# A fused attention and gated-MLP kernel: small steps moved off GpSimd, dependent pairs planned apart, tables offered to ScalarE

## The chip, the cores and the metric

The kernel runs on one core of one Trainium2 chip. The metric is the time of one execution in device microseconds; the time before is the median of three runs. A core has five instruction queues that matter here: TensorE (PE: matrix products, with its weight loads shown as PEld), VectorE (DVE), ScalarE (ACT), GpSimd (POOL) and SyncE (SP), which issues the DMA transfers. Each works through its own queue in order and waits on semaphores for the others.

## What is computed

Windowed causal attention with a distance penalty, whose output is the input of a gated MLP with a mix over the sequence. Batch 8, 8 heads, sequence 576, head size 64; model width 512, inner width 1024.

```python
scores = q @ k.T / sqrt(D) - slope[h] * (i - j)      # only 0 <= i - j < 128
attn = softmax(scores)
x = concat_heads(attn @ v)
u, v = split(relu(x @ w_in))
v_n = (v - mean(v)) / sqrt(var(v) + 1e-06)
out = (u * (w_spatial @ v_n + b_spatial)) @ w_out
```

## The kernel before, in words

The program is written as a list of pieces. Each piece (`plan.add`, `plan.either`) has an engine, or several to choose from, a weight (its planned time in ns), a due time, and the tiles that it reads and writes. `Plan.order` (L190) then simulates the engines with these weights: a piece that becomes ready goes to the engine whose queue, free time and weight end first (L207 to L211); a free engine takes the ready piece with the smallest number in the table `PLACES` (one three-digit hexadecimal number per piece, 2707 of them). `Plan.emit` (L259) writes the instructions out in that order, so the order on each engine is fixed before the program runs; no engine reorders anything. Where the simulated TensorE idles in the opening, `fill` (L388) puts matmuls of ones that compute nothing into a score bank (`x`, second buffer).

The work comes in stages that the plan overlaps:

- **Constants** (`constants`, L394). GpSimd writes the distances i - j of a tile (`relf`, and the transposed `relT`) in 64 rows; VectorE copies them to the other 64 (L401, L428). From them come eight tables `tabs` (L433 to L441, slope times distance, one per head; VectorE, and GpSimd from the third on, may make them) and eight transposed ones (L449, ScalarE or VectorE).
- **Opening attention** (`turned`, L740) for the four head pairs of batch 0 and two of batch 1. Scores go to PSUM (L720), VectorE adds the table and takes each row's extreme (L761), `split` (L764) cuts that number into three bf16 parts with two dependent subtractions (GpSimd or VectorE), TensorE transposes them (L779), and a second, transposed set of scores with table and maximum added by products (L791) gives the exponentials (L811). They are multiplied with v (L820); VectorE adds a small number to the row sums and inverts them (L847, L848, the second needs the first), and the output is scaled (L852 or L858), transposed (L865) and split into two f16 parts `xt` (L455, L877).
- **Attention of the other head pairs** (`scores`, `products`, `attention`, L893 to L1032): scores, table and extreme on VectorE (L914), exponentials (L920), division into two f16 parts (L952, L957), a DMA transpose (L963), and the products with v (L996).
- **Scales.** Weights and v are scaled by a power of two before they are cut into two f16 parts. `largest` (L640) finds the greatest sum of absolute values of v (L700 sums on ScalarE, one instruction per head pair); `scale_of` (L662) clamps it and multiplies it with two constants on GpSimd (L669, L670), then VectorE masks exponent bits (L672, L673). There are twelve scales: eight for v, four for weights (`column_scale`, L512).
- **Gated part** (`gated`, L1058), for each batch: products with w_in (L1081, L1103, L1132), the layer norm (`layer_norm`, L1038: statistics, their combination at L1046, variance plus epsilon at L1047, the power -1/2 on GpSimd at L1051, the normalization at L1055), the mix over the sequence (L1153), the gate, and the product with w_out (L1185).
- **Mixing weights** (`mixing_weights`, L578): the bias row is scaled into `r2` at rows 64 and 96, and its rounding error is put at row 96 (L633 to L636).

Of the kernel before, what the change touches and what calls it, by code (L numbers as in the profile page):

```python
# [21 lines left out]
def _as_f32(bits):  # L22
# [9 lines left out]
    "00000200100800501a00700400b0851e000601800901f01604301904203e06f03b07106007a05b07c00300c01201002e03005705003801401b01c02102202802702c02f034"  # L32
    "03903f08704404003c05905f04804f05405d06706c0700771991ad00a00e00d01100f01301501d01702301e02502402b02903102002602a03203302d03603a03d04a04c051"
    "05505a05205c06306606803704904104504704b04e06203504604d05305805606406106d07607d08408a08d08008608e09309505e06e06a06506b07307407906907207507e"
    "08107808c0830970a30b00b80bb0c00a50a80af0b20bd07b08208908f09209109b09d0c50ce0d20dd0e30e40d10d80df0e50e707f09609c0a2a920880900ad0b40c10c70b3"
    "0ae0e00b50c30bc0bf0c60cd0d40ca0d00db0e10e90ea0f10f70fa1d811511e13f1481041131020fc0ba0c40cc0d60f21011030ee0f80fb10010610810d1100fe10910e112"
    "11611a12412c0e80ed0f00f50fd10710b10511811d12712d1301361391111171201261d612b13313813c12313413714214a14e15315c13513e14414d15215615d160166168"
    "16914614f14b15713b13d14516717517f15416115e16a16416e17017c18718b14014314917217918117d18318218d1a21a818919119519b1d71961b01a51be1bb1c51c21c6"
    "1db19219f1b11b81981af1a31ae1b41ba1b61c41c11c81f71fa1c71e21ff2031d01e32001e71f822722b1f520b21f1fc20e22321022422922c21b22e24223124124e236246"
    "25124b2583402522633470f30990a009f0a40a70ac0ab0b70c20eb0ef0f41eb0f908b09409809e09a0a10a90a60b10b60b90be0c90c80cb0d50d70f610a10f11912212910c"  # L40
    "11b12112a12e0aa0cf0d30dc0d90da0de0e20e60ec0ff11411f12511c13212f13a15015b16c1e81fb1901ab1b51e51ec12813114c15115516315916b16216f14715815a174"
    "14115f17316d17816517617717b17e1801a01a419319419c1a119719d19e1aa1cd1b21c318a18c19a1cf1a91d91841881ee17117a1861a71d31da1851a61d11d51d41dc18f"
    "1b718e1ac1c91cc1d21ca1ce1bd1cb1e11e41e91f11e61ef1ea1f21ed1f41f01f620920721220a21320c21420420d20120f22f1f91fe20523923c23723a1b91df1bc1f31b3"
    "1fd1c021123324c26726c27546a1bf1dd20622520821822022d22223021621a21922a21e22621c22120221521721d23423823b23f24024723d24524824a24324925a24d253"
    "25b25f25e26025025925625c27123223524424f25525425727325d26d27827d28128628828b26a28428728a28c29129429a29e2a32a427728f29229829c2a12a52aa28e2a8"
    "2b22b62b92bf2c32c929f2af2b82bc2c12c62c82cd35c2ac2b72b42c02ba2c72c42d02cb2d92d32f232c3362de2fe2f930833233830331133333a30d31c31532634e351322"
    "34532a34f38c39034a35e38f39335736637436337239139536e37938e3763853a937e39839d3a038839f3af3a53b53d43ad3bb3d83b93d74943c13db49a1de228276280264"
    "26926226626527926827c27228226f27e26e27a26127026b27428528928d2902932962972a62992a029529d2bd2ad2b02be2c229b2a72a22a92ab2ae2d223e27b27f2832cc"
# [1268 lines left out]
```

## Time and profile before

| | before |
|---|---|
| median of three runs | 550.13 us (547.89 to 550.28) |
| the profiled execution's own time | 549.31 us |
| its span, first to last instruction | 547.6 us |
| busy: PE, DVE, ACT, POOL | 536.4, 444.2, 393.5, 61.5 us |
| mean granted TensorE clock | 1.000 of full speed |

Busy time is the time in which at least one instruction of an engine ran. The trace also lists, for each group of instructions, the idle time of the engine in front of it and which engine's instruction ended it, and a chain of waits that leads back from the last instruction to the first.

### The profile page before, as it was taken

What the parts mean: (1) busy time and instruction counts of PE and PEld (TensorE: products, weight loads), DVE (VectorE), ACT (ScalarE), POOL (GpSimd) and SP (SyncE); (2) the same over time, 40 slices, a digit from 0 to 9 for tenths busy, and PEclk for the clock granted to TensorE, in tenths of its full rate; (3) what the DMA queues carried; (4) which work ended last, traced back from release to release, by engine and by line L of the source; (5) the groups of instructions that cost most, each with busy time, mean ns of one, the idle gap of its engine ahead of it and who ended that gap; (6) DMA issues with size and microseconds to landing.
All of it is one profiled execution on the core that took longest, in us unless ns stands there. A gap on an engine that the chain in (4) does not pass through costs nothing.

```text
span 547.6 us, 19207 instructions
## 1 busy us (share of the span) xinstructions
PE 536.4 (98%) x7753; PEld 395.2 (72%) x7753; DVE 444.2 (81%) x1622; ACT 393.5 (72%) x1219; POOL 61.5 (11%) x138
## 2 busy tenths in 40 slices
PE   7898999999999999999999999999999999999997
PEld 6787567775678857886687758886688857884775
DVE  9788999999999799778998599858997799625540
ACT  4567799998978788569977699759976787323212
POOL 4011320212210011100100011100220011001000
PEclk9999999999999999999999999999999999999999
DMA  8949430489979975958498666965564744610002
GB/s 252 326 159 323 114 99 31 95 170 205 239 127 216 205 164 115 197 144 184 119 192 168 167 137 133 197 165 140 106 141 118 153 89 89 87 65 24 2 12 76
DMA packets 161405, 78.67 MB, mean 144 GB/s; under 512 B 124834, under 2 KB 155554, under 8 KB 161316
## 3 DMA queue, kind: packets, MB, share of 16 engines
q1 hardware_dynamic: 161316, 77.45, 62.4%
q8 instruction: 60, 0.98, 0.7%
q14 instruction: 29, 0.24, 0.1%
HBM read 37.13 MB, written 9.44 MB: 85 GB/s over the span
## 4 chain that ended last, share of the span: by engine, by line
PE 84%; DVE 6%; ACT 6%; issue 1%; DMA 1%; POOL 0%; DVEq 0%; ACTq 0%
PE m L1153 18%; PE m L1185 16%; PE m L1132 15%; PE m L1081 13%; PE s L720 8%; PE x L996 7%; PE s L791 2%; PE m L1103 2%; PE x L390 2%; DMA moved<-pq 1%; PE x L820 1%; ACT prob L920 1%; ACT prob L858 1%; ACT vt L459 1%; PE x L865 1%
## 5 line engine op out<-in xcount | busy, mean ns | idle before, releaser
L920 ACT ACTIVATE prob<-prob,stat 128x192 f32<-128x192 f32 (+1 forms) x260 | 109.3, 424 | 9.5 <-DVE stat L914 9.1
L1153 PE MATMUL m<-wsp,staged 128*128 128x288 f16 x768 | 113.2, 286 | 0.0
L1132 PE MATMUL m<-xt,win 128*128 128x288 f16 x768 | 100.1, 286 | 0.3 <-ACT vt L459 0.3
L1185 PE MATMUL m<-gs,wout 128*128 128x288 f16 x768 | 99.2, 286 | 0.0
L952 ACT ACTIVATE pq<-prob,stat 128x192 f16<-128x192 f32 (+1 forms) x260 | 88.8, 420 | 9.6 <-DMA moved<-pq 3.0
L957 DVE SCALAR_TENSOR_TENSOR pq<-prob,stat,pq 128x192 f16<-128x192 f32 (+1 forms) x260 | 87.8, 379 | 3.5 <-ACT pq L952 3.2
L1132 PEld LDWEIGHTS <-win 128*128 128x128 f16 x768 | 74.8, 98 | 21.8 <-issue 1.8
L1153 PEld LDWEIGHTS <-staged 128*128 128x128 f16 x768 | 74.2, 98 | 21.1 <-issue 2.5
L1185 PEld LDWEIGHTS <-wout 128*128 128x128 f16 x768 | 74.5, 98 | 20.3 <-issue 1.4
L914 DVE CUSTOM_DVE_ANT_0 prob<-s,tab 128x192 f32<-128x192 f32 (+1 forms) x260 | 71.6, 318 | 19.1 <-PE s L720 18.8
L1081 PE MATMUL m<-win,xt 128*128 128x512 f16 x384 | 86.3, 380 | 0.7 <-ACT o L1191 0.5
L1081 PEld LDWEIGHTS <-xt 128*128 128x128 f16 x384 | 36.4, 98 | 46.2 <-issue 5.4
L1051 POOL TENSOR_TENSOR st<-st,nhalf 128x1 f32<-128x1 f32 (+1 forms) x40 | 27.5, 687 | 296.5 <-DVE st L1047 290.3
L1161 DVE TENSOR_TENSOR u<-m,u 128x288 f32<-128x288 f32 x64 | 28.8, 449 | 35.2 <-PE m L1153 35.0
L720 PE MATMUL s<-qkraw 64*64 64x64 f32 (+1 forms) x1116 | 53.6, 313 | 1.5 <-DVE most L761 1.5
L920 ACT ACTIVATION_READ_ACCUMULATOR prob<-prob,stat 128x1 f32 (+1 forms) x260 | 49.6, 191 | 0.0
L1191 ACT ACTIVATE o<-m,am 128x288 f32<-128x288 f32 x41 | 20.2, 496 | 40.0 <-PE m L1185 32.8
L720 PEld LDWEIGHTS s<-qkraw 64*64 64x64 f32 x1116 | 40.3, 133 | 4.3 <-DVE most L761 1.9
L996 PEld LDWEIGHTS <-vh 128*64 128x64 f16 (+1 forms) x1664 | 34.6, 111 | 8.1 <-issue 6.6
L996 PE MATMUL x<-moved,vh 128*64 128x64 f16 (+1 forms) x1664 | 39.3, 197 | 0.1
L459 ACT ACTIVATE u<-m 128x288 f32<-128x288 f32 x54 | 21.7, 404 | 24.4 <-PE m L1132 24.1
L996 PE MATMUL x<-moved,vl 128*64 128x64 f16 (+1 forms) x832 | 37.4, 195 | 0.0
(167 smaller groups left out, 760.8 us busy)
## 6 DMA issues: line engine op xcount, KB each, us to landing
qkraw<-in_qk_dram SPq DMA_DIRECT2D x28, 576.0 KB, 4.3
vb<-in_v_dram SPq DMA_DIRECT2D x32, 320.0 KB, 5.7
out_dram<-o SPq DMA_DIRECT2D x64, 144.0 KB, 2.0
staged<-in_w_in_dram SPq DMA_DIRECT2D x8, 512.0 KB, 7.5
moved<-in_w_out_dram SPq DMA_DIRECT2D x4, 512.0 KB, 5.9
gw<-in_w_spT_dram SPq DMA_DIRECT2D x4, 288.0 KB, 7.5
moved<-pq SPq DMA_TRANSPOSE x52, 4.7
qkraw<-in_qk_dram SPq DMA_DIRECT2D x2, 320.0 KB, 4.6
```

Of the source, the lines that this page charges most:

```text
L720: nc.tensor.matmul(sc[j]()[out, at:at + k1 - k0], raw()[rows, 0, i * D:(i + 1) * D], raw()[rows, 1, k0:k1], start=True, stop=True, skip_gr ...
L914: nc.vector.tensor_tensor_reduce(pt(), sc[t][j]()[:m, SOFF[t]:SOFF[t] + n], tabs[h]()[:m, W - n:], -0.125, 3e38, ALU.add, ALU.min, st()[:m ...
L920: nc.scalar.activation(pt(), pt(), AF.Exp, bias=st()[:m, NM, j, t:t + 1], scale=-1.0, accum_out=st()[:m, SM, j, t:t + 1])
L952: nc.scalar.activation(pq[j]()[:m, 0, qs], prob[2 * (p % 2) + j]()[:m, cs], AF.Copy, scale=st()[:m, RC, j, t:t + 1])
L957: nc.vector.scalar_tensor_tensor(pq[j]()[:m, 1, qs], prob[2 * (p % 2) + j]()[:m, cs], st()[:m, RC, j, t:t + 1], pq[j]()[:m, 0, qs], ALU.mu ...
L996: nc.tensor.matmul(xp()[j * D:(j + 1) * D, x0:x0 + D], l()[rows, kt, j * D:(j + 1) * D], rhs, start=(i % 2, j) not in seen, stop=False, sk ...
L1051: nc.gpsimd.tensor_tensor(st()[:m, 11:12], st()[:m, 10:11], nhalf()[:m], ALU.pow)
L1081: nc.tensor.matmul(pt(), xt[c]()[:, X0[a] + t * P:X0[a] + (t + 1) * P], win()[:, c, w, DH:DF], start=(n == 0), stop=(n == 3 * NC_ - 1))
L1132: nc.tensor.matmul(pt()[:, :HS], win()[:, c, w, d * P:(d + 1) * P], xt[c]()[:, X0[a] + hf * HS:X0[a] + (hf + 1) * HS], start=(n == 0), sto ...
L1153: nc.tensor.matmul(pt()[:, :HS], l, r, start=(n == 0), stop=(n == len(ops) - 1))
L1161: nc.vector.tensor_tensor(u(), pt()[:, :HS], u(), ALU.mult)
L1185: nc.tensor.matmul(pt()[:, cs], wout()[:, d, w, e * P:(e + 1) * P], gs[d]()[:, a, cs], start=(n == 0), stop=(n == 3 * ND - 1))
```

## The change

Two subtractions of `split` and the two steps of `scale_of` move from GpSimd to VectorE. Pairs of small operations of which the second needs the first (in `split`, `scale_of`, after L820, and in the layer norm) become two pieces each, so that the plan can put other work between them. The copies of the distances and the eight tables may also go to ScalarE. For batches 1 to 7 the absolute sums of v take two head pairs per instruction, and `junk` doubles. The bias row lies at rows 64 and 65 instead of 64 and 96 and is scaled in one instruction. Some planned weights change, and the table of places has 2764 entries instead of 2707. In the diff unchanged lines and the table are left out.

```diff
@@ -29,65 +29,67 @@
...
@@ -358,7 +360,7 @@
-    junk = fixed([P, NQ * P], F16, "junk")
+    junk = fixed([P, 2 * NQ * P], F16, "junk")
@@ -398,7 +400,8 @@
-        plan.add("DVE", 500, 800, lambda: nc.vector.tensor_copy(relf()[D:], relf()[:D]), [(relf, 0)], [(relf, 1)])
+        plan.either([("DVE", 400, lambda: nc.vector.tensor_copy(relf()[D:], relf()[:D])), ("ACT", act(W), lambda: nc.scalar.copy(relf()[D:], relf()[:D]))],
+                    800, [(relf, 0)], [(relf, 1)])
@@ -425,7 +428,8 @@
-        plan.add("DVE", 575, 1000, lambda: nc.vector.tensor_copy(relT()[D:], relT()[:D]), [(relT, 0)], [(relT, 0)])
+        plan.either([("DVE", 400, lambda: nc.vector.tensor_copy(relT()[D:], relT()[:D])), ("ACT", act(W), lambda: nc.scalar.copy(relT()[D:], relT()[:D]))],
+                    1000, [(relT, 0)], [(relT, 0)])
@@ -438,7 +442,10 @@
-            plan.either([("DVE", 420, fv)] + [("POOL", pool(W), f)] * (h > 1), 1000 + h * 1000, [(relf, 0), (relf, 1)], [(tabs[h], 0)])
+            def fs(h=h):
+                slope = 2.0 ** (-8.0 * (h + 1) / H)
+                nc.scalar.activation(tabs[h](), relf(), AF.Copy, scale=-8.0 * slope)
+            plan.either([("DVE", 420, fv), ("ACT", act(W), fs)] + [("POOL", pool(W), f)] * (h > 1), 1000 + h * 1000, [(relf, 0), (relf, 1)], [(tabs[h], 0)])
@@ -485,7 +492,7 @@
-        return lambda: plan.add("DVE", dve(n), due + 3, f, [*W, X], [X])
+        return lambda: plan.add("DVE", dve(n) + 60, due + 3, f, [*W, X], [X])
@@ -589,7 +596,7 @@
-            nc.sync.dma_start(bt()[96:97, :], b_sp)
+            nc.sync.dma_start(bt()[65:66, :], b_sp)
@@ -630,11 +637,16 @@
-        def f():
-            for a in (64, 96):
-                nc.vector.tensor_scalar(r2()[a:a + 1, :], bt()[a:a + 1, :], sc(a, a + 1), None, ALU.mult)
-            nc.vector.scalar_tensor_tensor(r2()[96:97, :], bt()[96:97, :], sc(96, 97), r2()[96:97, :], ALU.mult, ALU.subtract)
-        plan.add("DVE", 1950, due + 2600, f, [(rest_, 1), (r2, 2), (r2, 1)] + ready, [(r2, 1)])
+        def fv():
+            nc.vector.tensor_scalar(r2()[64:66, :], bt()[64:66, :], sc(64, 66), None, ALU.mult)
+        def fa():
+            nc.scalar.activation(r2()[64:66, :], bt()[64:66, :], AF.Copy, scale=sc(64, 66))
+        plan.either([("DVE", 530, fv), ("ACT", act(S, 1), fa)], due + 2600, [(rest_, 1), (r2, 2), (r2, 1)] + ready, [(r2, 1)])
+        def f():
+            nc.vector.scalar_tensor_tensor(r2()[64:65, :], bt()[64:65, :], sc(64, 65), r2()[64:65, :], ALU.mult, ALU.subtract)
+        plan.add("DVE", dve(S, pointers=1) + 100, due + 2601, f, [(rest_, 1), (r2, 1)] + ready, [(r2, 1)])
@@ -666,9 +678,12 @@
-            nc.gpsimd.tensor_scalar(am()[:, 2:3], am()[:, col:col + 1], 2.0 ** -98, 2.0 ** 126, ALU.max, ALU.min)
-            nc.gpsimd.tensor_scalar(am()[:, 3:5], consts(), am()[:, 2:3], None, ALU.mult)
-        plan.add("POOL", 850, due, f, [(am, key), (consts, 0)], [(am, 3)])
+            nc.vector.tensor_scalar(am()[:, 2:3], am()[:, col:col + 1], 2.0 ** -98, 2.0 ** 126, ALU.max, ALU.min)
+        plan.add("DVE", 75, due, f, [(am, key)], [(am, 5)])
+        def f():
+            nc.vector.tensor_scalar(am()[:, 3:5], consts(), am()[:, 2:3], None, ALU.mult)
+        plan.add("DVE", 130, due, f, [(am, 5), (consts, 0)], [(am, 3)])
@@ -696,10 +711,13 @@
+        z = 2 if b else 1
+        for p in range(0, NP, z):
-                nc.scalar.activation(junk().rearrange("p (a b) -> p a b", b=P), vb()[:, p, :, 1:1 + P], AF.Abs, accum_out=am()[:, 8 + p:9 + p])
-            plan.add("ACT", act(NQ * P, 1), due + 8000 + p * 100, f, [(vb, p)], [(junk, 0), (am, ("sum", p))])
-        largest(am, [(am, ("sum", p)) for p in range(NP)], lambda: am()[:, 8:8 + NP], due + 9000, b < ONPE)
+                nc.scalar.activation(junk()[:, :z * NQ * P].rearrange("p (a b) -> p a b", b=P), vb()[:, p:p + z, :, 1:1 + P].rearrange("p c a b -> p (c a) b"), AF.Abs,
+                                     accum_out=am()[:, 8 + p // z:9 + p // z])
+            plan.add("ACT", act(z * NQ * P, 1), due + 8000 + p * 100, f, [(vb, p + k) for k in range(z)], [(junk, 0), (am, ("sum", p))])
+        largest(am, [(am, ("sum", p)) for p in range(0, NP, z)], lambda: am()[:, 8:8 + NP // z], due + 9000, b < ONPE)
@@ -761,10 +779,10 @@
-        def split(e):
-            for k in range(2):
-                e.tensor_tensor(ms()[:, :, :, k + 1], ms()[:, :, :, k], upper()[:, :, :, k], ALU.subtract)
-        plan.either([("DVE", 420, lambda: split(nc.vector)), ("POOL", 800, lambda: split(nc.gpsimd))], due + 2500, MS, [MR])
+        for k in range(2):
+            def split(k=k):
+                nc.vector.tensor_tensor(ms()[:, :, :, k + 1], ms()[:, :, :, k], upper()[:, :, :, k], ALU.subtract)
+            plan.add("DVE", 100, due + 2500 + k, split, MS if k == 0 else [MR], [MR])
@@ -845,8 +863,11 @@
+                plan.add("DVE", 110, d, f, [(xp, 0), (am, 4)], [(sm, 1)])
+                def f(sm=sm, nt=nt):
-                plan.add("DVE", 345, d, f, [(xp, 0), (am, 4)], [(sm, 0)])
+                plan.add("DVE", 105, d + 1, f, [(sm, 1)], [(sm, 0)])
@@ -1044,8 +1065,11 @@
+        plan.add("DVE", 100, due + 2, f, [(st, 0)], [(st, 3)])
+        def f():
-        plan.add("DVE", 335, due + 2, f, [(st, 0), (am, 12)], [(st, 1)])
+        plan.add("DVE", 110, due + 2, f, [(st, 3), (am, 12)], [(st, 1)])
@@ -1053,7 +1077,7 @@
-        plan.add("DVE", dve(DH, True, 2), due + 4, f, [(vt, 0), (st, 1), (st, 2)], [(vt, 0)])
+        plan.add("DVE", dve(DH, True, 2), due + 4, f, [(vt, 0), (st, 3), (st, 2)], [(vt, 0)])
```

## Rows read from the trace of the kernel before

**Rows 1.** The page, busy time: busy us, share of the span, instructions.
```profile
PE 536.4 (98%) x7753; PEld 395.2 (72%) x7753; DVE 444.2 (81%) x1622; ACT 393.5 (72%) x1219; POOL 61.5 (11%) x138
```

**Rows 2.** Stretches: from:to, length, busy us of each engine, PEclk, DMA share, GB/s.
```profile
0.00:60.00 60.00, 54.30 (x1125) 42.83 (x1126) 50.50 (x206) 36.51 (x80) 12.66 (x43) 1.00 0.86 267
60.00:120.00 60.00, 59.92 (x793) 43.06 (x795) 57.95 (x177) 56.83 (x165) 11.09 (x19) 1.00 0.35 82
120.00:480.00 360.00, 358.85 (x5285) 263.47 (x5278) 309.94 (x1179) 284.19 (x942) 34.99 (x72) 1.00 0.74 153
480.00:548.00 68.00, 63.36 (x561) 45.86 (x559) 25.85 (x62) 16.02 (x33) 2.78 (x5) 0.99 0.10 36
```

**Rows 3.** Line 390, the fillers: ns min/median/max, starts; idle before, by releaser.
```profile
L390 PE MATMUL x<-ones x131: 243/246/368, 1.3 to 58.2; 128*128 128x192 bf16 x131
...
  ACT prob L858: 1.4, 1
```

**Rows 4.** The chain of waits in order of time: start us, us, what.
```profile
43.46 1.81 PE x L390 x20
...
58.87 2.60 PE m L1081 x12
```

**Rows 5.** Timeline, 3 to 9 us: start, us, engine, line, operation, [idle before].
```profile
3.47 3.99 DVE L440 TENSOR_SCALAR tab<-u 128x192 bf16<-128x192 f32 x8
...
4.50 0.50 PE L720 MATMUL s<-qkraw 64*64 64x64 f32 x6
...
5.26 1.58 POOL L885 MEMSET pq<- 128x384 f16 x6
...
7.38 0.35 DVE L761 CUSTOM_DVE_ANT_0 s<-s,tab 128x192 f32<-128x192 f32 x1
...
8.67 0.74 ACT L700 ACTIVATE junk<-vb 128x640 f16<-128x640 f32 x1 [3.07 <-DMA vb<-in_v_dram]
...
8.84 0.58 PE L720 MATMUL s<-qkraw 64*64 64x64 f32 x3 [1.50 <-DVE most L761]
```

**Rows 6.** Lines 440 and 449, the tables: ns min/median/max, first and last start.
```profile
L440 DVE TENSOR_SCALAR tab<-u x8: 241/314/1809, 3.5 to 7.2; 128x192 bf16<-128x192 f32 x8
...
L449 ACT ACTIVATE gs<-u x8: 345/346/362, 3.5 to 5.3; 128x192 bf16<-128x192 f32 x8
```

**Rows 7.** Line 766, the splits: ns min/median/max; then busy us, mean ns.
```profile
L766 POOL TENSOR_TENSOR most<-most x10: 207/208/1235, 10.5 to 57.1; 128x10 f32<-128x10 f32 x10
...
L766 DVE TENSOR_TENSOR most<-most x2: 181/182/183, 13.3 to 13.5; 128x10 f32<-128x10 f32 x2
...
L766 POOL TENSOR_TENSOR most<-most 128x10 f32<-128x10 f32 x10 | 4.2, 421 | 30.1 <-DVE most L761 21.4 <-DVE sm L847 8.3
```

**Rows 8.** Scales: lines 669, 670, 672 (ns min/median/max); timeline at 40 us.
```profile
L669 POOL TENSOR_SCALAR am<-am x8: 209/229/971, 16.6 to 402.4; 128x1 f32<-128x1 f32 x8
...
L670 POOL TENSOR_SCALAR am<-powers,am x8: 313/314/2278, 16.9 to 403.5; 128x2 f32<-128x2 f32 x8
...
L672 DVE TENSOR_SCALAR am<-am x8: 132/144/155, 19.4 to 403.9; 128x1 int32<-128x1 int32 x8
...
39.97 0.31 POOL L670 TENSOR_SCALAR ham<-powers,ham 128x2 f32<-128x2 f32 x1
...
41.26 0.14 DVE L672 TENSOR_SCALAR ham<-ham 128x1 int32<-128x1 int32 x1
```

**Rows 9.** Timeline of VectorE at 67 us: two pairs, L847 and L848.
```profile
67.26 0.22 DVE L847 TENSOR_SCALAR sm<-x,am 128x6 f32<-128x6 f32 x1
67.52 0.19 DVE L848 RECIPROCAL sm<-sm 128x6 f32<-128x6 f32 x1
67.62 0.18 DVE L847 TENSOR_SCALAR sm<-x,am 128x4 f32<-128x4 f32 x1
```

**Rows 10.** Lines 700, 603 and 635: ns min/median/max, first and last start.
```profile
L700 ACT ACTIVATE junk<-vb x32: 719/734/824, 8.7 to 383.9; 128x640 f16<-128x640 f32 x32
...
L603 ACT ACTIVATE wsp<-gw x2: 1182/1188/1193, 48.4 to 50.3; 128x1152 bf16<-128x1152 f32 x2
...
L635 DVE TENSOR_SCALAR r<-moved,wam x2: 519/534/549, 64.8 to 65.4; 1x576 f16<-1x576 f32 x2
```

More of the change, by code (lines that the diff above doesn't have):

```diff
@@ L31 @@
 PLACES = (
[L32 to L47, printed above, removed]
@@ L88 @@
[L88 to L90 removed]
+    "00000400200601a01300300f01409c1fb00701b00801d01c04401704604107504007706608806408b00100901100e03903705905d03401502102502901e02702a02d031033"
@@ new lines @@
+    "03603a03b09d03d04e04a06c06905505c06807d07307608008419b1a400500d00a00b00c01201001601901802002202602402c02803e04201f02302b03002f02e035032038"
+    "03f04304805205806104c05005605b06206303c04904504d04b05105405706004704f05305a05f05e06a06707207907c07f08608f09307b08308508909009506506e06b06f"
+    "06d07407107a08207007807e08d08a08109209409709f0ad0b00bb0bf0c60a00a30aa0b80bc0c408708e09109b0a109a0a60a70cc0d50db0e30e60e90eb0d60d90e00e50ea"
+    "0ed08c09809e0a20abacb0a40960bd0c80c90cf0c70c30f30b50be0ba0c20cb0d10da0d40de0e20e70ef0f10f60f80fc1011f013213a15615e11412012a1301060d00d30d7"
@@ new lines @@
+    "0dd0e410d10f0f510310510910b1121171211220ff10e11111911d12612c1311360fa0fe10210710c11811b11312713313513913d14014714a12312812e1341381ef13c141"
+    "13e14612f14814e15415d16616c17717e14415015515f16316b16e17617c18518b18814d16515c1731531581611911a01a717018718318f18a19419319e1a91ad160162169"
+    "18618e19619a1ab1a51b01c81cf1af1b81bc1c31c61ed1c71d01d21d91d71e01de1e31f61b51c41c91cd1c21d11cb1d61e11e41d41dd1da1e61ff2071e21f220120b1eb1fd"
+    "21d1f720d22022c20220e22121922824022223723b23e22f24825c24325b26a24b26026f2652763672712883601040a90a50b20ac0b60c00ce0f40fb10010a2091100990a8"
@@ new lines @@
+    "0b30af0b70ae0b40b90c10c50ca0cd0d20d80dc0df0ee0ec10811511a12512b14b15111c11f12412d15215b0b10e10f70f20e80f00fd0f911611e12913713b14314513f14c"
+    "14f16417218c1a21ac1fe20417417817b18021821b14214915a17115916716f18917919217519716817f15718419817a19016a18118219519919d1a11a619f1a31ba1be1ae"
+    "1b21b91bb1e51a81aa1b31b61b11b41bf1c11cc1e820616d17d1ec1f318d1c51c01e719c1ca1e91ee1b71ce1bd1f51f81f11f41f91fa1df1ea1fc20020320f20821320c216"
+    "20521120a21522b22322d21a22421f22721c23022523124921721e2382532562512541d31d51d81dc21222a24d26726b27a28528a4a51db21022e23622623223a23f23d241"
@@ new lines @@
+    "23523c22923424424723323924224524624a24e25225525926226425d26325725f25a26127826c27027427b26926d26626827927d29224c24f25e26e27527227729827c290"
+    "29529c29f2a22a72aa2ad28d29e2a12a62a82ac2b22b72ba2c12c82c92962b12b52b92bd2c02c62ca2d02b32ce2e32ef2f12f62fc3003042c32d32f32f72f82fa2fe303305"
+    "3882d12da2d52e42dd2ff2e730630231330931b34c35131732231d32f34e35332933a35d36233434433f35e36c37134836e36437b3ad3b03723833bb3be37f38d3a8389395"
+    "3bd3c139239f3c739a3b63c33a23bc3c03c23bf3ca3e63c63d43f33cf3e83fc3d93f74b73ef4004bd21425028328928428f27328028128729329a28e29427f28c28629727e"
@@ L91 @@
+    "a21a12a16a1ba1ea259d49d79dca2ba2ca2da2ea27a2aa2fa48a4aa46a49a50a4ca51a52a54a56a57a59a5ba5ea4fa55a58a5aa5ca5fa61a62a64a67a69a6ba53a60a63a66"
+    "a68a6aa6ca6ea70a5da6da73a75a76a79a7fa82a85a65a71a78a7aa7ca7da80a84a86aa5a6fa74a72a7ba77a81a7ea87a83a89a88a8ba97a98a8aa8da8ca8fa9aa9da8ea91"
+    "a9ba9fa90a93a92a95a9eaa0a94a99a96aa1ab2ab5a9caa4ab4ab8aa2aa8aafaa6aaaab6abaaa9aadab7aabab0abeaaeab3ab9abcab1abbac1abdabfac4ac0ac2ac7ac3ac5"
+    "ac9ac6ac8aca"
 )
```

83 lines of the change are left out of this document (40 added, 43 removed).

## The prediction, made before the changed kernel was run

> **What bounds the kernel now.** I read the busy times first: TensorE (PE) is busy for 536.4 us of a span of 547.6, VectorE (DVE) for 444.2 [rows 1]. So only what TensorE wastes can be won. The table of stretches says where that is [rows 2]. TensorE idles 5.70 us before 60 us, 0.08 from there to 120, 1.15 to 480, and after 480 it is busy 63.36 of the 67.6 us left (4.24, mostly the last output). The granted clock is full throughout (1.00; 0.99 in the last stretch), so the clock carries no term. Busy is not useful, though: line 390 holds filler matmuls that compute nothing, 131 of them, the last at 58.2 us [rows 3]. In the chain of waits 20 of them take 1.81 us [rows 4], 0.09 each, so 131 take about 11.9 us. From 58.87 us the first large matmul group of the gated stage (L1081) follows [rows 4], and fillers end. What can be won before 60 us is thus at most 5.7 + 11.9 = 17.6 us, later perhaps 1.2. The opening stage decides, and in it VectorE, 50.50 us busy of 60, is the fullest engine beside TensorE [rows 2].
>
> **Tables.** In the order of time, VectorE makes eight tables in 3.99 us from 3.47 us on, and touches the first scores (L761) only at 7.38, though TensorE produced six of their matmuls from 4.50 on [rows 5]. The second head pair's scores wait until 8.84 us, the last 1.50 us of it for L761 [rows 5]. One of the eight tables took 1809 ns against a median of 314 [rows 6]; beside it GpSimd (POOL) clears the probability buffers (L885, 1.58 us from 5.26) [rows 5]. After the change the planner (L207 to 211) gives each piece to the engine whose queue plus weight ends first. ScalarE (ACT) has weight 255 and VectorE 420. If both were empty, the eight go by that sum: table 0 to ScalarE (255 against 420), 1 to VectorE (420 against 510), 2 and 3 to ScalarE (510 against 840, 765 against 840), 4 to VectorE (840 against 1020), 5 to ScalarE, 6 to VectorE, 7 to ScalarE: three stay on VectorE. Three at 314 ns are 0.94 us from 3.47, done by 4.4, before the clearing starts. The first L761 is then limited by its scores: 4.50 + 0.50 = 5.0, say 5.2 with the hop. The two copies in front (L401, L428) may go the same way; the scores' load hides them. Gain at this point 7.38 - 5.2 = 2.2 us. ScalarE pays five tables of about 346 ns, 1.7 us [rows 6], and it idles in this stretch: the first sum over v starts at 8.67, after 3.07 us without work [rows 5]. The cover is that idle time; without it the 1.7 us would delay row copies. What is late next is data: the second pair's scores need their load and their score banks, the sums need v. So of 2.2 us at the start I carry 1.8 to the 58.87 us mark; ends: 0 (a later load or VectorE itself eats it) and 2.2.
>
> **Splits of the maxima (L766).** Ten instructions in five pieces ran on GpSimd, at 207 to 1235 ns (median 208), and two on VectorE, 181 to 183 ns [rows 7]. All twelve go to VectorE: ten times 0.18 = 1.8 us added there, all before 58 us. Removed is a detour over GpSimd in front of the transposes at L779: two operations of 421 ns on the mean [rows 7], 0.84 us, where VectorE needs 0.36. Each split now also queues behind VectorE's own work. I take the latency saved as 0.3 of that 0.48, 5 x 0.3 = 1.5 us, against 1.8 us of VectorE time, of which half falls into its idle 9.5 us (60 - 50.5): 0.6 saved net; ends: -1.8 (no latency saved, all on the path) and +2.4 (five times 0.48, at no cost). On GpSimd only the powers of the layer norm, the constants of the scales and the opening's memsets stay; nothing is queued behind what leaves.
>
> **Scales (L669, L670).** Twelve pairs leave GpSimd: 209 to 971 and 313 to 2278 ns for the eight v scales [rows 8]. They become two VectorE operations each of about 0.14 us (nearest row: L672, one column) [rows 8]: 24 x 0.14 = 3.4 us on VectorE, 0.6 of it before 58 us (two pieces). For the weights' scale GpSimd works to 40.28, and L672 starts only at 41.26 since VectorE was busy with L761 [rows 8]: the hop was hidden behind VectorE's own queue, so I take nothing for it; ends -0.6 and +1.0 (the 0.98 from 40.28 to 41.26). SP's queue keeps its transfers: one bias row lands on partition 65 instead of 96.
>
> **Dependent pairs.** L847 starts at 67.26, the reciprocal that needs it 0.26 later, and the next independent L847 0.10 after that, before its predecessor has ended [rows 9]. So a pair with other work between can save up to 0.16 us: eight pairs before 60 us, 1.3 us; the planner fills perhaps half of them with work: 0.7 us, ends 0 and 1.3. Forty pairs in the layer norm (L1046, L1047), up to 6.4 us of VectorE, lie after 58.87 us, where TensorE is covered; nothing. The Trainium skill, VectorE: DVE Perf Modes, section "The DRAIN you can't avoid", speaks against this term: it says that the next operation cannot issue until the pipe is empty, and that a semaphore in between costs nothing extra. By it separating the pair saves zero, and the sum below would be 0.7 us smaller; the starts in this trace overlap, which that sentence does not describe.
>
> **Edits that cost nothing here.** For batches 1 to 7 the sums over v take two head pairs per operation: 28 operations of 734 ns [rows 10] become 14; a 1152-column operation on the same engine takes 1188 ns [rows 10], 1280 columns by that 1.32 us, so 14 x (1.47 - 1.32) = 2.1 us less on ScalarE and 14 reads of the accumulator; TensorE, full after 60 us, hides it. A sum now waits for two loads, with the exponentials queued behind it on ScalarE; between 60 and 120 us ScalarE is busy 56.83 of 60 [rows 2], so this cover is thin there, and a late load would show as a wait of TensorE, in the ends of the next sentences but one. Of the bias rows' two scalings (519 and 549 ns [rows 10]) one stays, about 0.5 us less at 65 us, under TensorE. New weights and a new table of places reorder everything after 60 us. Idle there can shrink by 1.2 us; a bad meeting can cost as much as one that the trace shows: TensorE waited 1.4 us for ScalarE's L858 [rows 3] and then ran 1.81 us of fillers [rows 4], 3.2 together. I take 0, ends -3.2 and +1.2.
>
> **The sum.** Saved: 1.8 + 0.6 + 0 + 0.7 + 0 = 3.1 us of the profiled execution's 549.31 (span 547.6 plus 1.7 around it): 546.2. The three runs have a median of 550.13, 0.8 above it, so the forecast is 547.0 for the median, 0.6% faster. A measurement here can tell about 0.5%, 2.75 us.
>
> **Rivals.**
> - No net effect. VectorE works 50.5 of 60 us before and gives up 3.05 us of tables (3.99 - 0.94), but takes on 1.8 of splits and 0.6 of scales: 0.65 us freed. If its throughput, or a load, sets 58.87 us, and not its late start, the gain is 0.65 us: 549.5. Tables that the planner keeps on VectorE after all, so that the edit doesn't do what it says, end here too. For it: 50.5 of 60. Against it: 9.5 us of idle there. Chance 0.34 for within 0.5%.
> - A tighter opening. With the small latencies gone the new order needs half of the 17.6 us of fillers and idle: 8.8 less, 541.3. For it: every filler run stands in front of one of the small steps. Against it: the order of the large pieces changes little. Chance 0.16.
> - A held filler. Fillers write the second x bank and must wait for whoever reads it, as they did 1.4 us for L858 [rows 3], with 20 of them behind it [rows 4]. Their number is fixed from planned, not real times. If the new plan puts one more such meeting on the path and the tables gain nothing, that is +3.2: 553.3. It decides as soon as wait and fillers exceed what the opening gains: one such meeting cancels the forecast's 3.1, two make it slower. For it: it happens before the change [rows 3]. Against it: once in 131. Chance 0.12.
>
> **How the numbers follow.** Forecast with its own range of 543.5 to 547.3: 0.38; tighter opening 0.16; no net 0.34; slower 0.12. Faster by over 0.5%: 0.38 + 0.16 = 0.54; within: 0.34; slower: 0.12. The range for 8 in 10 runs from 541.3 (the tighter opening; beyond it 0.07) to 552 (two thirds of the way to the held filler, beyond it 0.08).
>
> **What would show it.** Right: first L761 near 5.2 us, the first L1081 2 to 4 us before 58.87, fewer fillers than 131, GpSimd with no L766 or L669, TensorE without idle from 60 to 480 us. Wrong: tables still on VectorE until 7 us; an early first L761 but L1081 again at 58 to 59 us (then the bound is a load or VectorE); new waits of TensorE for VectorE after 60 us, where VectorE is 57.95 us busy of 60 [rows 2].

## The result, and the profile after

The changed kernel takes 553.0 us (median of six runs, 552.41 to 555.45) where the kernel before takes 550.06 (six runs, the three of the table before among them): the ratio is 1.0072, 95% interval 1.0045 to 1.0099. It is slower by 0.7%, where 0.6% faster was forecast. Its profiled execution took 552.43 us, with a span of 550.2 against 547.6. Line numbers shift: fillers are now L392, scores L738, extremes L779, splits L784, transposes L797, the product with v L838, sums and reciprocals L865 and L869, w_in's products L1105 and L1156, the power L1075.

The page's busy times answer to [rows 1]:

```profile
PE 538.3 (98%) x7768; PEld 397.2 (72%) x7768; DVE 444.3 (81%) x1656; ACT 389.0 (71%) x1190; POOL 54.1 (10%) x104
```

VectorE has taken over what left GpSimd and is no busier: 444.3 us against 444.2. The table of stretches answers to [rows 2]:

```profile
0.00:60.00 60.00, 54.64 (x1128) 44.16 (x1129) 47.25 (x210) 37.22 (x81) 6.47 (x27) 1.00 0.85 266
60.00:120.00 60.00, 60.00 (x772) 42.69 (x770) 58.66 (x189) 54.95 (x156) 8.53 (x12) 1.00 0.35 83
120.00:480.00 360.00, 358.23 (x5301) 262.85 (x5295) 312.17 (x1197) 280.18 (x920) 35.57 (x60) 1.00 0.74 154
480.00:550.00 70.00, 65.45 (x578) 47.54 (x576) 26.19 (x64) 16.64 (x34) 3.48 (x5) 1.00 0.10 35
```

Before 60 us VectorE has 3.25 us less to do (50.50 to 47.25) and TensorE idles 0.34 us less (5.70 to 5.36); still the first product with w_in stands in the chain of waits 0.2 us later than at 58.87 [rows 4]:

```profile
59.08 5.18 PE m L1105 x24
```

Behind 60 us TensorE idles 6.5 us where it was 5.5. The fillers and TensorE's list of waits answer to [rows 3]:

```profile
L392 PE MATMUL x<-ones x146: 242/246/368, 1.3 to 70.8; 128*128 128x192 bf16 x146
```

```profile
PE m L1156 <- ACT vt L466: 1.0, 3, 0.4
PE m L1209 <- ACT o L1215: 1.0, 1, 1.0
PE x L392 <- DVE prob L873: 0.9, 1, 0.9
PE x L392 <- DVE most L779: 0.8, 1, 0.8
PE x L392 <- ACT xt L462: 0.5, 1, 0.5
```

There are 15 fillers more, about 1.4 us of work; with the idle time that is some 2.1 of the 2.6 us that the span grew. Three groups of fillers wait for a reader of their bank, 2.2 us in all, where one waited 1.4. (One wait is put down to an extreme, L779, which reads another bank; ScalarE's normalization L879 out of the fillers' bank ends 0.01 us before it.) The start of the timeline answers to [rows 5] and [rows 6]:

```profile
2.46 1.63 ACT L447 ACTIVATE tab<-u 128x192 bf16<-128x192 f32 x6
2.63 0.54 DVE L444 TENSOR_SCALAR tab<-u 128x192 bf16<-128x192 f32 x2
4.81 1.38 PE L738 MATMUL s<-qkraw 64*64 64x128 f32 x14
6.34 0.37 DVE L779 CUSTOM_DVE_ANT_0 s<-s,tab 128x192 f32<-128x192 f32 x1 [1.64 <-PE s L738]
8.17 0.50 PE L738 MATMUL s<-qkraw 64*64 64x64 f32 x6
```

Six tables are ScalarE's, done by 4.1 us. The first extreme starts 1.04 us earlier, and the second pair's scores 0.67 us (8.84 to 8.17). The small operations answer to [rows 7], [rows 8] and [rows 10]:

```profile
L784 DVE TENSOR_TENSOR most<-most x12: 167/172/183, 9.6 to 67.4; 128x10 f32<-128x10 f32 x12
L681 DVE TENSOR_SCALAR am<-am x8: 140/146/155, 15.7 to 393.4; 128x1 f32<-128x1 f32 x8
L685 DVE TENSOR_SCALAR am<-powers,am x8: 198/221/228, 16.2 to 402.7; 128x2 f32<-128x2 f32 x8
L717 ACT ACTIVATE junk<-vb x18: 737/1258/1385, 9.5 to 381.4; 128x1280 f16<-128x1280 f32 x14, 128x640 f16<-128x640 f32 x4
```

**Where the time goes.** One stretch can be compared exactly, since TensorE does the same useful work in it in both kernels: from the product with v of batch 0's third head pair (or batch 1's first scores, whichever comes first) to the transposes of batch 1's first pair. It is called the third pair's stretch below. In the timeline of TensorE in the kernel before it begins and ends with

```profile
38.58 0.45 PE L720 MATMUL s<-qkraw 64*64 64x64 f32 x6
...
46.20 0.54 PE L779 MATMUL s<-ident,most 64*128 64x64 bf16 x5
```

which is 7.62 us; in the changed kernel with

```profile
37.97 1.93 PE L838 MATMUL x<-vb,prob 128*64 128x65 f32 x65
...
42.21 0.98 PE L392 MATMUL x<-ones 128*128 128x192 bf16 x10 [0.82 <-DVE most L779]
...
43.88 0.98 PE L392 MATMUL x<-ones 128*128 128x192 bf16 x10 [0.46 <-ACT xt L462]
...
45.45 2.22 PE L392 MATMUL x<-ones 128*128 128x192 bf16 x25
47.60 0.54 PE L797 MATMUL s<-ident,most 64*128 64x64 bf16 x5
```

which is 9.63 us, 2.0 longer: it begins 0.6 us earlier and ends 1.4 us later. 45 fillers stand in it instead of 22. What VectorE does meanwhile shows its timeline:

```profile
40.01 0.36 DVE L865 TENSOR_SCALAR sm<-x,am 128x6 f32<-128x6 f32 x2 [0.69 <-PE x L838]
40.28 0.75 DVE L541 TENSOR_SCALAR win<-wx,ham 128x1024 f16<-128x1024 f32 x1
40.94 0.25 DVE L869 RECIPROCAL sm<-sm 128x4 f32<-128x4 f32 x2
...
45.31 0.17 DVE L784 TENSOR_TENSOR most<-most 128x10 f32<-128x10 f32 x1
45.39 1.28 DVE L546 SCALAR_TENSOR_TENSOR win<-wx,ham,win 128x1024 f16<-128x1024 f32 x1
46.59 0.18 DVE L784 TENSOR_TENSOR most<-most 128x10 f32<-128x10 f32 x1
```

The pairs are set apart as the change wants it, but by large operations: the reciprocals wait for one of 0.75 us, the second half of the split for one of 1.28 us, and the transposes need that half. It is done at 46.77 us, and the 25 fillers planned ahead of the transposes hold TensorE until 47.6.

### The profile page after: what moved, and what is told of

Its sections match the earlier page's. It is cut to its first block, busy times and chain, and to the rows that moved or that the text cites. A ratio compares the mean times of both kernels' runs of the same rounds, so it can differ in the third digit from the quotient of the medians.

```text
span 550.2 us, 19197 instructions
## 1 busy us (share of the span) xinstructions
PE 538.3 (98%) x7768; PEld 397.2 (72%) x7768; DVE 444.3 (81%) x1656; ACT 389.0 (71%) x1190; POOL 54.1 (10%) x104
## 4 chain that ended last, share of the span: by engine, by line
PE 84%; DVE 8%; DMA 3%; issue 1%; ACT 1%; POOL 1%; SPq 1%; ACTq 0%; POOLq 0%; DVEq 0%
PE m L1177 20%; PE m L1156 16%; PE m L1209 15%; PE m L1105 11%; PE s L738 8%; PE x L1017 6%; PE x L392 2%; PE s L809 2%; PE m L1127 2%; DMA out_dram<-o 1%; DVE st L1063 1%; PE x L838 1%; DVE pq L978 1%; DMA staged<-in_w_in_dram 1%; DMA moved<-in_w_out_dram 1%
## 5 line engine op out<-in xcount | busy, mean ns | idle before, releaser
L1156 PE MATMUL m<-xt,win 128*128 128x288 f16 x768 | 100.8, 286 | 1.2 <-ACT vt L466 1.0
L1156 PEld LDWEIGHTS <-win 128*128 128x128 f16 x768 | 74.5, 98 | 23.3 <-issue 3.7
L1105 PE MATMUL m<-win,xt 128*128 128x512 f16 x384 | 86.8, 379 | 0.9 <-issue 0.8
L1105 PEld LDWEIGHTS <-xt 128*128 128x128 f16 x384 | 36.4, 98 | 46.2 <-issue 5.8
L1075 POOL TENSOR_TENSOR st<-st,nhalf 128x1 f32<-128x1 f32 (+1 forms) x40 | 34.6, 865 | 320.8 <-DVE st L1071 303.3
L738 PE MATMUL s<-qkraw 64*64 64x64 f32 (+1 forms) x1116 | 53.9, 316 | 0.0
L466 ACT ACTIVATE u<-m 128x288 f32<-128x288 f32 x57 | 22.9, 403 | 29.4 <-PE m L1156 29.2
L738 PEld LDWEIGHTS s<-qkraw 64*64 64x64 f32 x1116 | 40.7, 134 | 2.9 <-issue 1.3
L1063 DVE BATCH_NORM_STATS2 st<-vt 128x6 f32<-128x512 f32 (+1 forms) x40 | 27.4, 686 | 12.9 <-ACT vt L466 12.8
```

Of the source, the lines that this page charges most:

```text
L738: nc.tensor.matmul(sc[j]()[out, at:at + k1 - k0], raw()[rows, 0, i * D:(i + 1) * D], raw()[rows, 1, k0:k1], start=True, stop=True, skip_gr ...
L1063: nc.vector.bn_stats(st()[:m, 0:6], vt()[:m])
L1075: nc.gpsimd.tensor_tensor(st()[:m, 11:12], st()[:m, 10:11], nhalf()[:m], ALU.pow)
L1105: nc.tensor.matmul(pt(), xt[c]()[:, X0[a] + t * P:X0[a] + (t + 1) * P], win()[:, c, w, DH:DF], start=(n == 0), stop=(n == 3 * NC_ - 1))
L1156: nc.tensor.matmul(pt()[:, :HS], win()[:, c, w, d * P:(d + 1) * P], xt[c]()[:, X0[a] + hf * HS:X0[a] + (hf + 1) * HS], start=(n == 0), sto ...
```

## The experiments

Four theories stood against each other. A: pairs set apart let large VectorE operations in between, which delays the chains of the opening. B: the new order of the large pieces and its fillers cost. C: the work added on VectorE costs. D: each edit by itself helps or is neutral, and the plan's new order (with what it does to GpSimd's powers) costs. All ratios are to the kernel before on the same chip; a difference between two experiments is taken from their ratios, times 549.5 us. Each execution also has a mean granted clock of TensorE, which is 0.999 or 1.0 for all six of the changed kernel. In some executions of most kernels it is 0.990 to 0.997, and they are longer: of the 23 of the kernel before beside a_pool, 21 took 548.49 to 550.93 us, and the two at 0.997 took 552.25 and 552.29. Where this bears on a comparison, it is said. Two edits that were made in the tables of numbers are given in words.

**Undoing parts in the changed kernel.** a_tied writes the second half of each pair directly behind the first:

```diff
-            self.ops[n][0][k][2]()
+            if n not in self.tied:
+                self.ops[n][0][k][2]()
+            if n + 1 in self.tied:
+                self.ops[n + 1][0][ways[n + 1]][2]()
```

> The changed kernel, with the second operation of every separated pair (splits, row sums, layer norm, scales) written out directly behind the first; nothing else moves, all engines and fillers as changed. Theory A (the pairs set apart let large VectorE operations in between, and the value comes late): the transposes' operand at 46.8 us comes 1.2 us earlier, the layer norm's powers shorter, time 551 to 552 (1 to 2 us below the changed kernel's 553.0). Theory B (the order of the large pieces and the fillers is what costs): within 0.5 us of 553.0. Theory C (VectorE's added work costs): within 0.5 us of 553.0.

Measured: 555.65 us, 1.0125 (1.0094 to 1.0156). Its page and first wait:

```profile
PE 539.7 (97%) x7765; PEld 397.2 (72%) x7768; DVE 449.7 (81%) x1656; ACT 389.5 (70%) x1190; POOL 51.4 (9%) x104
```

```profile
PE m L1165 <- ACT vt L470: 2.2, 4, 1.0
```

VectorE is 5.4 us busier than in the changed kernel, and TensorE waits 2.2 us for copies of `vt` instead of 1.0. So separating does save VectorE time, and under the new order that time seems to count (2.9 us, with intervals that overlap), which no theory had expected. The loss lies behind the opening: a_tied's first product with w_in starts 0.63 us earlier (58.28 against 58.91 in the timelines), and its span is 3.4 us longer. A as the whole cause falls.

a_nofill leaves out the fillers planned behind 36 us, in the changed kernel; b_nofill does it in the kernel before:

```diff
-            self.fill(fills)
+            self.fill(fills if now < 36000 else 0)
```

> The changed kernel without the 63 fillers that the plan puts behind 36 us of its own time; the fillers compute nothing, the output is the same. Theory B (fillers planned too long stand in front of ready work): the 4 us of them between 42 and 48 us shrink to what the data need, TensorE starts L1105 1 to 2 us earlier, 551 to 552. Theories A and C: the gap stays as idle time, 552.5 to 553.5; more if the granted clock falls behind the gaps.

> The kernel before without the 50 fillers that the plan puts behind 36 us of its own time. If fillers stand in front of ready work there too: 548 to 549.5; if not: 550 with the gaps as idle time; more if the granted clock falls behind the gaps.

Measured: 555.53 us, 1.0111 (1.0078 to 1.0145), and 550.66 us, 1.0025 (1.0014 to 1.0037). b_nofill is slower than with them; a_nofill is too, though the intervals overlap. In a_nofill the third pair's stretch shrinks to 7.81 us, so the fillers do stand in its way there; but its table of stretches shows what they were for:

```profile
36.00:48.00 12.00, 8.62 (x207) 6.85 (x208) 10.97 (x41) 7.32 (x20) 0.80 (x3) 0.93 0.72 241
48.00:60.00 12.00, 11.18 (x208) 8.91 (x209) 8.20 (x26) 9.06 (x17) 0.00 (x0) 0.79 0.86 273
```

TensorE idles 3.38 us of the first stretch, and the mean granted clock of the next is 0.79, so TensorE ran partly at its lower level (1.2 of 2.4 GHz). All ten executions of b_nofill have a mean granted clock of 0.994 to 0.997, all four of a_nofill 0.990 to 0.997.

a_pool gives splits and scales back to GpSimd within the new order; a_sums takes one sum per head pair again:

```diff
-            nc.vector.tensor_scalar(am()[:, 2:3], ...)
+            nc.gpsimd.tensor_scalar(am()[:, 2:3], ...)
```

> The changed kernel with the splits (six pieces of two) and the two steps of the twelve scales written for GpSimd again; the plan, the order on every other engine and the fillers stay as changed. Theory C (VectorE's added 5 us of small operations cost the time): 550.5 to 552. Theory D (the plan's order and fillers, or the layer norm's powers, cost; the move itself helps or is neutral): 553 or more, each hop to GpSimd and back adding up to 0.5 us in the opening.

> The changed kernel with one absolute sum of v per head pair again for batches 1 to 7 (28 instructions instead of 14, in the places of the 14); all else as changed. If the doubled sums cost time by waiting for two loads: 551 to 552.5. If they save ScalarE time that TensorE waits for: 553.5 to 555. Else within 0.5 us of 553.0.

Measured: 553.13 us, 1.0062 (1.0042 to 1.0081): within the noise the move neither costs nor wins, and C falls. And 555.13 us, 1.0102 (1.0085 to 1.0119): the merged sums look worth 1.6 us there, though the interval overlaps the changed kernel's. a_oldorder carries the old table of places over to the new pieces and lets the plan run again:

```diff
(in words)
-PLACES = (... 2764 new entries ...)
+PLACES = (... each piece the entry it had before, halves the same one ...)
```

> The changed kernel with the old table of places carried over piece by piece (both halves of a separated piece get the place of the whole). Theory B (the new order costs): as the kernel before or up to 1.5 us faster, 548.5 to 550. Theories A and C (the edits cost): 552 to 554 or more.

Measured: 557.48 us, 1.0165 (1.0135 to 1.0195), with 162 fillers. The old table doesn't give the old order, because the planned weights decide readiness; so this run says nothing about the old order itself.

**Single edits in the order of the kernel before.** b_dve has splits and scales on VectorE (a_pool's edit reversed), b_tabs the tables 0, 2, 3, 5 and 7 on ScalarE, both with the old order and fillers:

```diff
-                nc.vector.tensor_scalar(tabs[h](), relf(), -8.0 * slope, None, ALU.mult)
+                if h in (1, 4, 6):
+                    nc.vector.tensor_scalar(tabs[h](), relf(), -8.0 * slope, None, ALU.mult)
+                else:
+                    nc.scalar.activation(tabs[h](), relf(), AF.Copy, scale=-8.0 * slope)
```

> The kernel before with the splits and the two steps of the scales written for VectorE; its order and its fillers stay. Theory C: 551 to 553. Theory D: 548 to 550, at most as the kernel before.

> The kernel before with five of the eight tables (0, 2, 3, 5, 7) written for ScalarE, three left on VectorE; order and fillers stay. If the opening sets the end: first L761 near 6 us and the time 0.9 us lower, 548.5 to 549.3. If what is gained at the start is waited for later: within 0.4 us of the kernel before.

Measured: b_dve 549.69 us, 1.0003 (0.9991 to 1.0016), neutral a second time; b_tabs 548.27 us, 0.9982 (0.9974 to 0.9991), faster by 1.0 us. b_apart adds to b_dve that the second half of every pair waits for the next VectorE operation; b_three joins b_dve, b_tabs and the merged sums; b_all is both together:

```diff
+            if any(d in self.ops[n][2] for d, _ in late):
+                ...
             g = self.ops[n][0][k][2]()
+            if self.ops[n][0][k][0] == "DVE":
+                for _, h in late:
+                    h()
```

> The kernel before with its own order and fillers; splits and scales on VectorE, and the second half of every dependent pair (splits, steps of the scales, sum and reciprocal, spread and its scaling) written behind the next VectorE operation that the order has, unless a reader of the pair comes first. Theory A (pairs set apart let large VectorE operations in between and so delay the chains): VectorE's busy time falls by 3 to 6 us but the time is 551 to 553 us. Theory D (the new order of the large pieces costs, setting pairs apart helps): 547.5 to 550 us, VectorE's busy time 3 to 6 us less.

> The kernel before with its own order and fillers; tables 0, 2, 3, 5 and 7 on ScalarE, splits and scales on VectorE, and from the second batch on one sum of v's magnitudes per two head pairs. Theory D (every edit by itself helps or is neutral): 546.5 to 548.5 us, at least the 1 us of the tables. Rival (the edits compete for the same cover on VectorE and ScalarE once they are together): 549.5 to 552 us.

> All of the two: the kernel before with its own order and fillers and nearly every edit of the change (tables, splits, scales, merged sums, pairs set apart; the bias rows left as they were). It differs from the changed kernel in the order and the fillers. Theory D (order costs): 545 to 548.5 us, so 4 us or more below the changed kernel. Theories A and C (the edits themselves cost): 551 to 554 us.

Measured: 551.42 us, 1.0041 (1.0024 to 1.0059); 548.94 us, 1.0000 (0.9985 to 1.0014); 552.1 us, 1.0047 (1.0033 to 1.0061). So the tables' 1.0 us is not seen in b_three (the intervals overlap), and D's "helps or is neutral" holds for three of the edits together only as neutral. In the old order setting the pairs apart is what costs, 2.1 us (b_apart against b_dve) and 2.6 (b_all against b_three), although VectorE becomes 4.2 us less busy (446.5 in b_three, 442.3 in b_all). Part of it comes with a lower clock: b_apart's five executions at 0.999 or 1.0 took 550.47 to 551.17 us and all twelve of b_dve 549.2 to 550.64; b_all has one, 551.74, above all ten such of b_three (547.99 to 550.52). The third pair's stretch shows 0.5 of the 2.1 us. It takes 7.80 us in b_dve and 8.31 in b_apart; in b_apart's timelines of VectorE, ScalarE and TensorE (in this order):

```profile
43.27 0.35 DVE L861 TENSOR_SCALAR sm<-x,am 128x6 f32<-128x6 f32 x2
...
44.65 0.17 DVE L862 RECIPROCAL sm<-sm 128x4 f32<-128x4 f32 x1
```

```profile
44.93 0.93 ACT L872 ACTIVATE prob<-x,sm 128x64 f32<-128x64 f32 x4 [0.56 <-DVE sm L862]
```

```profile
45.91 1.81 PE L403 MATMUL x<-ones 128*128 128x192 bf16 x20 [2.04 <-DVE prob L866]
```

Two extremes got in front of the second reciprocal, ScalarE waits 0.56 us for it, and the fillers wait 2.04 us where they wait 1.53 in b_dve. In b_all the same group of 20 took far longer than the 1.81 us of [rows 4], shown by TensorE's timeline and the stretch around it:

```profile
43.11 3.36 PE L403 MATMUL x<-ones 128*128 128x192 bf16 x20 [2.04 <-ACT prob L879]
```

```profile
43.00:47.00 4.00, 3.89 (x25) 3.40 (x24) 1.42 (x4) 0.17 (x2) 0.00 (x0) 0.57 1.06 313
```

After the 2.04 us idle TensorE ran them at a mean granted clock of 0.57, mostly at the lower level; that is 1.55 of the 2.1 us by which the stretch grew (9.94). In b_apart the same idle was followed by the full clock. There it had fallen earlier (0.50 from 24 to 26 us), behind the idle time near 20 us that all these kernels have, and the profiled execution (553.15 us) is 1.7 above the median; where the rest of the 2.1 us lies was not found.

**Two orders by two stretches.** Three kernels contain every edit and differ only in order, fillers and choice of engine: h_all follows the kernel before throughout (halves side by side), h_open follows it up to the first matmul of the batches' own work (58.8 us) and the changed kernel behind it, h_rest the reverse. The order is written out as a list:

```diff
-        end, out = self.order(self.links(False), due, True)
-        for n, k, *_, fills in out:
+        for at in range(0, len(places), 6):
+            n, k, fills = (int(places[at + i:at + j], 16) for i, j in ((0, 3), (3, 4), (4, 6)))
```

> All edits of the changed kernel; up to the first matmul of the batches' own work (about 58.8 us) in the order and with the fillers of the kernel before, halves of pairs side by side there; behind it in the changed kernel's order. If the opening's order loses what the traces show (the changed kernel falls back by 2.3 us between 34 and 55 us): 550 to 551.5 us. If the loss lies in the order behind the opening: 552.5 to 554 us.

> All edits; the opening in the changed kernel's order and with its fillers, everything behind it in the order of the kernel before, halves side by side there. If the opening's order costs 2.3 us and nothing else: 551 to 552.5 us. If the order behind the opening costs too: below 551 us; if it is worth something: over 553 us.

> All edits, the whole in the order and with the fillers of the kernel before, halves of pairs side by side. If the edits by themselves are neutral or help: 547.5 to 549.5 us, and the whole difference to the changed kernel is order and the halves' separation. If the edits cost: over 551 us.

| opening | behind it | us | ratio (95%) | executions at a mean clock of 0.999 or 1.0, us | third pair's stretch, us |
|---|---|---|---|---|---|
| before's | before's (h_all) | 549.71 | 1.0001 (0.9988 to 1.0014) | 9 of 12: 548.06 to 550.37 | 7.80 |
| before's | changed (h_open) | 551.0 | 1.0031 (1.0018 to 1.0044) | 10 of 11: 550.01 to 552.2 | 7.80 |
| changed | before's (h_rest) | 553.32 | 1.0069 (1.0041 to 1.0096) | 1 of 6: 551.02 | 9.63 |
| changed | changed (the change) | 553.0 | 1.0072 (1.0045 to 1.0099) | 6 of 6: 552.41 to 555.45 | 9.63 |

With every edit in, the order decides (with it go the halves' places and the order of the loads). By the medians the opening's order costs 2.3 us (h_open to the change) or 3.7 (h_all to h_rest), and the order behind it 1.6 us behind the old opening (h_all to h_open) and 0.2 behind the new one. But h_rest is a poor witness: five of its six executions have a mean granted clock of 0.993 to 0.997. Its profiled one has 0.83 from 20 to 30 us, and a wait of the transposes at the seam of the two orders, which is in the lists of waits of neither h_all nor the change, with a second fall behind it (TensorE's timeline and the stretch):

```profile
62.85 0.77 PE L855 MATMUL s<-ident,most 64*128 64x64 bf16 x5 [1.69 <-DVE most L842]
```

```profile
60.00:70.00 10.00, 8.31 (x108) 0.83 0.25 62
```

Its one execution at the full clock, 551.02 us, lies between h_all and the change, as two costs that add would have it; one is too few to show it. For the part behind the opening the list of TensorE's waits in h_open has a line

```profile
PE m L1214 <- ACT vt L524: 2.3, 4, 1.0
```

for the u products, which in h_all is

```profile
PE m L1214 <- ACT vt L524: 0.3, 1, 0.3
```

so there small waits for a copy are 2.0 us longer. These are single executions, and whether the halves' separation or the order of the large pieces makes the waits was not taken apart. b_best sets pairs apart only behind the opening, in the old order, with b_three's edits:

```diff
+                if now < 50000:
+                    g()
+                else:
+                    late.append((n, g))
```

> The kernel before's order and fillers; tables on ScalarE, splits and scales on VectorE, merged sums, and pairs set apart only behind the opening. If setting pairs apart costs only in the opening, where a chain of single operations ends before TensorE can go on: 546.5 to 548.8 us, a time below that of both kernels. If it costs in the later batches too: 550 to 552 us.

Measured: 550.96 us, 1.0029 (1.0016 to 1.0043), where b_three has 1.0000. I expected a time below both kernels. That setting apart costs 1.6 us behind the opening as well is not shown. Six of the twelve executions have a mean granted clock of 0.996 or 0.997 (551.0 to 552.58 us); the other six took 549.23 to 550.93. In the profiled one the clock fell between 22 and 26 us, ahead of the first pair that is set apart (50 us of planned time) and behind 1.57 us of idle time; b_three idles 1.41 us there and keeps the full clock. The stretch in b_best, then in b_three:

```profile
22.00:26.00 4.00, 4.00 (x72) 0.57 0.98 273
```

```profile
22.00:26.00 4.00, 4.00 (x91) 1.00 1.09 284
```

The first product with w_in starts at 59.45 us in b_best and 58.76 in b_three, and the spans are 549.2 and 548.7: behind the opening b_best loses nothing in these two executions.

**Which piece of the opening.** a_open1 is the changed kernel with halves side by side in the opening and 5 instead of 25 fillers ahead of the transposes at 47.60; a_open2 also gives the largest normalization of the third pair back to VectorE (the plan had sent all ten to ScalarE):

```diff
(in words)
-  piece 422 (transposes): 25 fillers; halves at their own places
+  piece 422 (transposes): 5 fillers; each half directly behind its first, up to 50 us planned
```

> The changed kernel with two marks of its opening taken back: halves of pairs side by side up to the batches' own work, and 5 instead of 25 fillers ahead of the transposes of batch 1's first pair. If the split set around a 1.28 us operation and the fillers planned for it hold TensorE there (25 fillers took 2.22 us): 551 to 552 us. If what holds it is the work ahead (the normalization of the third pair's probabilities, ten operations on ScalarE, 2.16 us): 552.5 to 553.5 us.

> As the last, and the largest of the third pair's normalizations on VectorE, where the kernel before has it, in the place of the changed kernel's order. If the plan's choice of engine holds TensorE between 34 and 55 us: 0.5 to 1.2 us under the last. If VectorE, which has ten extremes to do behind it, is then the one that is late: the same or slower.

Measured: a_open1 551.52 us, 1.0044 (1.0024 to 1.0064); a_open2 553.06 us, 1.0072 (1.0047 to 1.0096). In a_open1 the stretch is back at 7.64 us, in TensorE's timeline:

```profile
37.98 1.94 PE L896 MATMUL x<-vb,prob 128*64 128x65 f32 x66
...
45.12 0.57 PE L450 MATMUL x<-ones 128*128 128x192 bf16 x5
45.62 0.54 PE L855 MATMUL s<-ident,most 64*128 64x64 bf16 x5
...
47.02 1.88 PE L896 MATMUL x<-vb,prob 128*64 128x65 f32 x64 [0.85 <-DVE xt L956]
```

It begins where it did and ends 1.98 us earlier; 0.85 us goes to a new wait for `xt`, and 1.5 us are left by the ratios, with intervals that overlap. Its eight executions at a mean clock of 0.999 or 1.0 took 550.51 to 552.74 us (median 551.2), the change's six 552.41 to 555.45 (median 553.0). Halves side by side alone left it at 9.29 us (a_tied, where the 25 fillers still ran), no fillers alone at 7.81 (a_nofill, where the transposes waited 1.7 us for the split). So the set-apart split and the fillers planned for it hold this stretch together; that this is most of what the opening loses is likely, not shown. Nothing speaks for the engine of the normalization as a cause: in a_open2 the stretch is 7.64 us as well. Its longer time proves little, since four of its six executions have a clock of 0.994 to 0.997; the other two took 551.28 and 552.44 us, as a_open1 does.

No run has a lower ratio than b_tabs, 0.9982: it is faster than both kernels.

## Why the prediction was wrong

- **What bounds.** Right in part: the opening decides 2.3 of the 3.9 us that the order costs. Its waste was read as a reserve of 17.6 us from which savings are drawn. It is also what a new order can add to, and 2.0 us were added in one stretch. I had named an early first extreme with the first product of w_in still near 58.87 as the sign that a load or VectorE bounds, and that is what came (6.34 and 59.08 us). The chain of waits does run over two weight loads from 40.51 to 51.37 us, but no wait of TensorE, VectorE, ScalarE or GpSimd from 20 to 60 us is put down to a load in either kernel.
- **Tables.** Direction right, size too large. I put the first extreme at 5.2 us and carried 1.8; it came at 6.34, since its scores ended late (1.38 us for the group that took 0.80 before; why was not found), and b_tabs is worth 1.0 us (0.5 to 1.4 from its interval). Two tables stay on VectorE, where the working had three.
- **Splits and scales.** 0.6 for the splits, 0 for the scales: two runs, one in each order, show nothing (a_pool, b_dve). The term was too large by its own size, within its ends. A scale's two steps take 0.15 and 0.22 us on VectorE, not 0.14 each.
- **Dependent pairs.** The step "the planner fills perhaps half of them with work: 0.7 us" failed in its sign. What stood between the halves was a large operation or an extreme, and it delayed a chain for which TensorE waited: b_apart is 2.1 us slower than b_dve. For the pairs behind 58.87 us the size was near, up to 6.4 us of VectorE against 5.4 measured over all pairs (a_tied), but "nothing" looks wrong: side by side costs about 2.9 us in the new order (a_tied, opening included, intervals overlapping), so TensorE is not covered there in every order; in the old order no cost of apart is shown there (b_best). The Trainium skill, VectorE: DVE Perf Modes, section "The DRAIN you can't avoid", says that the next operation cannot issue until the pipe is empty; by that sentence the separation would leave VectorE's time unchanged, and the 5.4 us (444.3 to 449.7) speak against it for these small operations. The same section adds that a next operation that is not held starts earlier, which the prediction left out.
- **Edits at no cost.** "I take 0, ends -3.2 and +1.2" for the new order is the step that decided. It was meant for what lies behind 60 us; the opening's new order had no term, so a loss there stood at nothing without a reason. Measured with all edits in: -2.3 for the opening and -1.6 behind it, which is within the ends, 3.9 together (1.0001 to 1.0072). The halves' separation is part of both, and how much of them it makes stays open. I had argued from what each edit does and let the order, which a plan makes anew for all 2764 pieces, stand at zero. The merged sums were taken as nothing; in the new order they look worth 1.6 us, with intervals that overlap.
- **The sum.** Of the 3.1 us saved none is seen when the edits are joined in the old order (b_three 1.0000, h_all 1.0001).
- **The rivals.** No net effect describes the edits in the old order (h_all), not the change. The held filler named 553.3 us with a chance of 0.12, and the time is 553.0; that it is so near is partly luck. Its mechanism is half right: three filler groups wait instead of one, and 25 fillers stood in front of the transposes. But the tables did gain (b_tabs), and taking all late fillers away doesn't help (a_nofill): the gap stays and the clock falls. The order was more than a chance meeting, so 0.12 was too little.

## What to carry to other kernels

A table of places fitted to one list of pieces is part of the kernel: an edit that is neutral or better by itself (tables, moves) can lose with a new order, and the new order must be priced by a run with the old order kept. Two dependent operations side by side are slower for their engine and sooner for the one that waits for them; set them apart only where nobody waits, and look at what the plan puts between. Fillers planned from one estimate hold the engine when the estimate is off, and without them the clock fell here (0.79 in a_nofill); shorten the gap first. Compare times at the same granted clock: in b_best a fall that came in six of twelve executions went with 2 us (medians 552.1 and 550.1), as much as the effects sought.

## What was not expected of the hardware

GpSimd's power of one column per partition in the layer norm is no fixed cost: over its 40 it takes 541 to 1590 ns before (median 580) and 541 to 1726 after (median 668). The timelines of GpSimd before and after, for corresponding places, have

```profile
444.02 0.57 POOL L1051 TENSOR_TENSOR st<-st,nhalf 128x1 f32<-128x1 f32 x1 [37.04 <-DVE st L1047]
```

```profile
445.64 1.73 POOL L1075 TENSOR_TENSOR st<-st,nhalf 128x1 f32<-128x1 f32 x1 [36.30 <-DVE st L1071]
```

and beside the second VectorE ran

```profile
446.07 0.87 DVE L1004 SCALAR_TENSOR_TENSOR vl<-vb,am,vh 128x640 f16<-128x640 f32 x1
447.40 0.55 DVE L1079 TENSOR_SCALAR vt<-vt,st 128x512 f32<-128x512 f32 x1 [0.47 <-POOL st L1075]
```

so VectorE itself waited 0.47 us for it. The Trainium skill, GPSIMD Engine Reference, section "Key points", says that GpSimd shares its SBUF interfaces with VectorE and that there is contention with VectorE's operations of two SBUF inputs; the operation at 446.07 (0.87 us) has such inputs, and the trace agrees as far as two places can. No run changed the powers alone, so what they cost the kernel is not shown.
